# Sinkhorn attention and a feed-forward block on one core: zero halves moved from q to K, and batch 0 without padding

## The chip, the cores and the metric

The kernel runs on one core of a Trainium2 chip. A core has a matrix engine, TensorE (PE), with its own stream of weight loads (PEld); VectorE (DVE); ScalarE (ACT); GpSimd (POOL); and SyncE (SP), which here only issues transfers. TensorE reads SBUF, the 128-partition working memory, and writes PSUM, 8 banks of 512 fp32 columns per partition. VectorE and ScalarE copy results out of PSUM. POOL and SP issue the DMAs: loads that turn fp32 into bf16 come from POOL, transposes and stores from SP.

The metric is the device time of one execution in microseconds (us). The profiles show single executions, with a span from the first to the last instruction; the time of the execution is slightly longer than its span.

## The reference, cut to what matters

```python
# q, k, v: (4, 8, 768, 64); sort_net: (4, 8, 8, 8); 8 blocks of 96 rows
P = sort_net
for _ in range(5):                     # sinkhorn
    P = exp(P - max(P, -1)); P = P / (sum(P, -1) + 1e-9); P = P / (sum(P, -2) + 1e-9)
k_sorted = einsum('bhij,bhjcd->bhicd', P, k_b)      # blocks of K and V mixed by P
v_sorted = einsum('bhij,bhjcd->bhicd', P, v_b)
scores = q_b @ k_sorted.T / 8                       # inside each 96-row block
attn = softmax(scores)
x = (attn @ v_sorted) -> (3072 tokens, 8 heads * 64 = 512)
h = x @ w_in                                        # 512 -> 2048
g = maximum(h, 0) + alpha * minimum(h, 0)
out = g @ w_out                                     # 2048 -> 512
```

## The kernel before

The kernel records its operations in a graph (`G.add`), each with the tiles that it reads and writes. Each engine then runs its own fixed sequence, given as lists of operation numbers (`ORDER`) together with the PSUM bank of each result (`BANKS`); both lists were found by a search. Semaphores are set where an operation needs another engine's result. An engine runs its list strictly in order, so an operation that waits holds up all behind it. "Fillers" in TensorE's list (L1009) and the burst (L907) are matmuls without a result that keep TensorE working while it would wait.

**Blocks.** There are 32 attention blocks g (4 batches b of 8 blocks i), each of 96 queries and keys for 8 heads. Heads stand in 4 pairs, h4 = 0..3 with the halves hp = 0, 1: half 0 in partitions 0 to 63 and half 1 in 64 to 127.

**Sinkhorn** (L560 to L574) is a chain of small VectorE operations with one ScalarE exponential per round. Its result Pb is spread by small matmuls (`spread0`, L584, for batch 0; `spread` for the others) and made into the mixing matrices BDQ, BDM (for K) and BDV (for V).

**Batch 0 ("near").** q is transposed by TensorE (`prep_q`, L645) and copied to QTz. `prep_k0` (L661) mixes and transposes K, in six units, each copied to KT. `prep_v` (L716) mixes V in eight units, each copied to VS. In KT each 24-key group is padded to 32 columns with copies of other keys (L670, on POOL), so that 96 keys become 128 columns; in VS the rows that belong to padding are zero, also in the column that counts the keys (`one0`). For V the tile hT serves as the loading area, with zeros at L495 and L497; the weights of `prep_v` are read from it with a step of 64 elements. A block then runs on TensorE as: s1 (L755: scores with the queries along partitions), a VectorE reduction to the negative maxima nm (L762), s2 (L770: scores with the keys along partitions), sub (L781: subtract the maximum), on ScalarE the exponential to ET (L801), on TensorE o (L812: outputs and the sums), on VectorE the reciprocal (L817) and product xq (L820), on TensorE the transpose tr (L834) and a copy to xT.

**Batches 1 to 3 ("far").** q is loaded by POOL head by head to QN (L430), 128 columns per head, of which the half of the other partition half is zero (QN0, L508). SP transposes QN (L440) to QTz, in six pieces of 1024 columns, so QTz holds two copies per pair with zero halves. `conv_k` (L677, POOL) and `prep_k` (L689) mix K; one copy per unit brings both halves into KT, 112 columns per pair and block. `conv_v` lays V into VDz, and `prep_v` mixes it. In a far block s1 (L752) is 8 matmuls of 96 moving columns: with 128 partitions and zero halves in the weights, each gives the scores of one head. VectorE takes the negative maxima nf, ScalarE the exponentials to Esb (L789), SP transposes Esb to ET (L794). There are NE = 3 buffers of Esb, ET and xq. For batches 2 and 3 SP transposes xq to xT too.

**Feed-forward.** FFN1 (L853) runs on two chunks of 192 tokens and then seven of 384, 16 tiles each: 4 matmuls, ScalarE's relu t (L860), VectorE's product and sum hT (L863). FFN2 (L885) runs per 128 tokens in four groups of 4 matmuls with 512 columns; VectorE or ScalarE copies the result to outstg and SP stores it (L896). A copy out of PSUM that both engines can do has the line of the helper, L397.

Of the kernel before, what the change touches and what calls it, by code (L numbers as in the profile page):

```python
# [13 lines left out]
NB = 8  # L14
# [9 lines left out]
BK = (128, 112)  # L24
LK = 4 * NB * 128
NE = 3
VSL = 4
EPS = 1e-9
BURST = 140
# [13 lines left out]
        723 759 662 894 659 893 890 660 661 889 663 819 787 788 818 918 917""",  # L43
    "sync": """
# [3 lines left out]
        1127 1098 1118 1090 1058 1148 1172 1214 1226 1193 1220 1232""",  # L48
    "pe": """
# [17 lines left out]
        1224 1217 1218 1229 1230""",  # L67
    "act": """
# [10 lines left out]
        1180 1183 1195 1198 1147 1204 1207 1225 1219""",  # L79
    "dve": """  # L80
# [13 lines left out]
        1163 1151 1178 1160 1187 1192 1166 1175 1171 1184 1202 1181 1196 1199 1208 1205 1213 1231""",  # L94
}
BANKS = (
    "0720176402566007103123674545623016702014516040740232332571154023556674710151666723230371765023127466"
    "7345562601566762045563520172323073704233472267005451247552145562703761201777760440167073416745102212"
    "4567503020451227731314512700026654567764370120171140356567274267567010450223343406134451717670102147"
    "562372753011225033452370700112467116304617335716342532617524"  # L100
# [221 lines left out]
def bass_sinkhorn_attn__then__act_prelu_kernel(  # L322
# [40 lines left out]
    one0 = sb("one0", [128, 1], F32)  # L363
# [6 lines left out]
    QN = sb("QN", [128, 6, 8, 128], BF16)  # L370
# [3 lines left out]
    QTz = [sb("QTz%d" % n, [128, 2, 4, S], BF16) for n in range(2)]  # L374
# [38 lines left out]
    d_qn = [dma_sem("qn%d" % h) for h in range(H)]  # L413
# [10 lines left out]
    def load_q(b, prio):  # L424
        if b == 0:
            o, i = quarters(hT, 8192, HR, q)
            G.add(POOL, lambda e: e.dma_start(o, i), load_us, w=[("QS", 0)], prio=prio, dma=(d_q, 0), kind="load")
            return
        for h in range(H):
            G.add(POOL, lambda e, h=h: e.dma_start(  # L430
                AP(QN, h * 128 + (h // 4) * 64, [[6144, 128], [1024, 6], [1, 64]]),
                AP(q.tensor, b * HB + h * S * D, [[D, 128], [128 * D, 6], [1, D]])),
                660, r=[("QN0", h)] + paced(13, h // 2) * (b == 3), w=[("QN", h)], prio=prio,
                dma=(d_qn[h], 0), kind="load")
# [45 lines left out]
    def consts():  # L480
# [26 lines left out]
        for h in range(H):  # L507
            G.add(POOL, lambda e, h=h: e.memset(  # L508
                AP(QN, h * 128 + (1 - h // 4) * 64, [[6144, 128], [1024, 6], [1, 64]]), 0.0),
                430, w=[("QN0", h)], prio=-21)  # L510
# [538 lines left out]
```

## Time and profile before

| | |
|---|---|
| times of the runs | 237.92, 237.5 and 244.82 us; median 237.92 |
| profiled execution | 237.91 us, span 236.2 us |
| granted TensorE clock, mean over the span | 0.986 |
| HBM read, written | 27.28 MB, 6.29 MB |
| DMA issues, median to landing: KS (768 KB) 9.8 us, w_in (512 KB) 9.2 us, QN (96 KB) 3.7 us | |
| DMA transposes, median to landing: QTz 3.4 us, ET 3.2 us, xT 2.4 us | |

Busy times are unions of an engine's instruction spans; instructions of one engine overlap by some hundredths of a microsecond, so a sum of durations is a little larger. For TensorE a matmul's duration contains the time it takes to run through the array, so what it costs in a dense stream is the distance from one start to the next, which the chain of waits shows (so many matmuls in so many us). The chain follows back from the last instruction what released each step.

### The profile page before, as it was taken

What the parts mean: (1) busy time and instruction counts of PE and PEld (TensorE: products, weight loads), DVE (VectorE), ACT (ScalarE), POOL (GpSimd) and SP (SyncE); (2) the same over time, 40 slices, a digit from 0 to 9 for tenths busy, and PEclk for the clock granted to TensorE, in tenths of its full rate; (3) what the DMA queues carried; (4) which work ended last, traced back from release to release, by engine and by line L of the source; (5) the groups of instructions that cost most, each with busy time, mean ns of one, the idle gap of its engine ahead of it and who ended that gap; (6) DMA issues with size and microseconds to landing.
All of it is one profiled execution on the core that took longest, in us unless ns stands there. A gap on an engine that the chain in (4) does not pass through costs nothing.

```text
span 236.2 us, 5977 instructions
## 1 busy us (share of the span) xinstructions
PE 228.7 (97%) x2379; PEld 144.9 (61%) x2379; DVE 167.2 (71%) x344; ACT 151.8 (64%) x421; POOL 104.3 (44%) x153
## 2 busy tenths in 40 slices
PE   5999989999999999999999999999999999999995
PEld 3469868866566666566665666565655556455553
DVE  5774499997699788896797687684877558634741
ACT  4356648988598796687867758457758564433331
POOL 7939929997399997431778880000000000000000
PEclk9998599999999999999999999999999999999999
DMA  5999999996999999999828999842282691400024
GB/s 82 213 218 208 208 190 209 220 153 46 179 181 132 106 127 181 220 231 180 160 80 84 102 132 143 164 81 51 60 118 75 154 166 44 140 4 0 0 92 179
DMA packets 72381, 31.35 MB, mean 133 GB/s; under 512 B 64528, under 2 KB 67360, under 8 KB 72352
## 3 DMA queue, kind: packets, MB, share of 16 engines
q0 software_dynamic: 23808, 13.63, 42.6%
q1 hardware_dynamic: 48544, 17.33, 36.8%
q8 instruction: 19, 0.31, 0.6%
q14 instruction: 10, 0.08, 0.1%
HBM read 27.28 MB, written 6.29 MB: 142 GB/s over the span
## 4 chain that ended last, share of the span: by engine, by line
PE 82%; DMA 7%; DVE 5%; ACT 3%; issue 1%; SPq 0%; POOLq 0%
PE ps L853 32%; PE ps L885 31%; PE ps L716 4%; PE ps L752 4%; PE ps L812 3%; DMA ET<-Esb 3%; DMA hT<-in_q_dram 3%; PE ps L781 2%; DVE hT L863 2%; PE ps L689 1%; ACT ET L801 1%; DVE outstg L397 1%; PE ps L834 1%; PE ps L755 1%; DMA out_dram<-outstg 1%
## 5 line engine op out<-in xcount | busy, mean ns | idle before, releaser
L863 DVE SCALAR_TENSOR_TENSOR hT<-t,omaT,ps 128x384 bf16<-128x384 f32 (+1 forms) x144 | 76.7, 562 | 30.8 <-ACT t L860 29.1
L853 PE MATMUL ps<-xT,w_in_bf 128*128 128x384 bf16 (+1 forms) x576 | 95.6, 308 | 0.2 <-DVE rec L817 0.2
L885 PE MATMUL ps<-w_out_bf,hT 128*128 128x512 bf16 (+1 forms) x400 | 93.4, 371 | 0.1
L860 ACT ACTIVATE t<-ps 128x384 f32<-128x384 f32 (+1 forms) x144 | 61.5, 458 | 43.8 <-PE ps L853 33.7
L853 PEld LDWEIGHTS ps<-xT,w_in_bf 128*128 128x128 bf16 x576 | 51.8, 98 | 29.6 <-ACT xT L397 0.4
L885 PEld LDWEIGHTS ps<-w_out_bf,hT 128*128 128x128 bf16 x400 | 36.5, 98 | 32.9 <-DVE VS L397 0.2
L789 ACT ACTIVATE Esb<-ps,nf 96x96 bf16<-96x96 f32 x192 | 46.1, 345 | 6.4 <-DVE nf L762 6.2
L397 POOL COPY VDz<-VST 64x384 bf16<-64x384 bf16 x40 | 34.1, 852 | 9.8 <-DMA VST<-in_v_dram 6.0
L677 POOL COPY KSz<-KS 64x512 bf16<-64x512 bf16 x36 | 22.0, 612 | 8.9 <-DMA KS<-in_k_dram 3.6
L762 DVE TENSOR_REDUCE nf<-ps 96x8 f32<-96x768 f32 x24 | 22.7, 948 | 3.5 <-PE ps L752 3.4
L430 POOL DMA_DIRECT2D QN<-in_q_dram x24 | 20.0, 838 | 6.5 <-DMA QTz<-QN 6.5
L820 DVE TENSOR_TENSOR xq<-ps,rec 96x512 bf16<-96x512 f32 x32 | 21.7, 681 | 0.4
L812 PEld LDWEIGHTS ps<-VS,ET 112*128 112x128 bf16 (+1 forms) x256 | 11.4, 99 | 5.2 <-ACT ET L801 0.9
L812 PE MATMUL ps<-VS,ET 112*128 112x65 bf16 (+1 forms) x256 | 13.4, 196 | 1.1 <-ACT ET L801 0.6
L397 DVE COPY outstg<-ps 128x512 f32<-128x512 f32 (+1 forms) x14 | 9.3, 667 | 7.1 <-PE ps L885 4.8
L752 PEld LDWEIGHTS ps<-KT,QTz 128*96 128x96 bf16 x192 | 11.9, 125 | 3.6 <-ACT VS L397 0.5
L397 ACT ACTIVATE VS<-ps 112x512 bf16<-112x512 f32 (+1 forms) x18 | 12.0, 697 | 3.1 <-PE ps L716 2.9
L397 ACT ACTIVATE KT<-ps 128x512 bf16<-128x512 f32 x17 | 9.8, 600 | 4.1 <-PE ps L661 2.4
L752 PE MATMUL ps<-KT,QTz 128*96 128x96 bf16 x192 | 12.4, 208 | 0.0
L817 DVE RECIPROCAL rec<-ps 96x8 f32<-96x8 f32 x32 | 6.3, 200 | 8.3 <-PE ps L812 8.1
L762 DVE TENSOR_REDUCE nm<-ps 96x8 bf16<-96x768 f32 x8 | 7.6, 949 | 5.9 <-PE ps L755 5.8
L397 ACT ACTIVATE outstg<-ps 128x512 f32<-128x512 f32 (+1 forms) x11 | 6.4, 579 | 7.9 <-PE ps L885 7.9
(101 smaller groups left out, 183.6 us busy)
## 6 DMA issues: line engine op xcount, KB each, us to landing
out_dram<-outstg SPq DMA_DIRECT2D x23, 256.0 KB, 2.6
KS<-in_k_dram POOLq DMA_DIRECT2D x3, 768.0 KB, 9.8
QN<-in_q_dram POOLq DMA_DIRECT2D x24, 96.0 KB, 3.7
w_in_bf<-in_moe_w_in_dram POOLq DMA_DIRECT2D x4, 512.0 KB, 9.2
w_out_bf<-in_moe_w_out_dram POOLq DMA_DIRECT2D x2, 1024.0 KB, 16.3
VST<-in_v_dram POOLq DMA_DIRECT2D x4, 384.0 KB, 13.5
hT<-in_q_dram POOLq DMA_DIRECT2D x1, 768.0 KB, 7.3
hT<-in_v_dram POOLq DMA_DIRECT2D x2, 384.0 KB, 6.2
```

The lines of the kernel that those rows point to most:

```text
L397: return e.activation(o, i, ACTF.Copy) if e is nc.scalar else e.tensor_copy(o, i)
L430: G.add(POOL, lambda e, h=h: e.dma_start(AP(QN, h * 128 + (h // 4) * 64, [[6144, 128], [1024, 6], [1, 64]]), AP(q.tensor, b * HB + h * S * ...
L677: G.add(POOL, lambda e, hp=hp: e.tensor_copy(AP(KSz, hp * 64 * 3072 + u % 3 * 1024 + hp * 64, [[3072, 64], [128, 8], [1, 64]]), AP(KS[n], ...
L752: inst = e.matmul(o, AP(QTz[n], hp * 3072 + h4 * 768 + i * 96, [[6144, 128], [1, 96]]), AP(KT[n], (h4 * 8 + i) * bk, [[LK, 128], [64, 2], ...
L762: G.add(DVE, lambda e: e.tensor_reduce(AP(nx, 0, [[8, 96], [4, 2], [1, 4]]), AP(ps, X.at(), [[LP, 96], [X.step, 2], [96, 4], [1, 96]]), Ax ...
L789: inst = e.activation(AP(Esb[me], p * 128, [[1024, 96], [64, 2], [1, 48]]), AP(ps, X.at((p % 4) * 96) + p // 4 * X.step, [[LP, 96], [48, 2 ...
L812: inst = e.matmul(AP(ps, Z.at(h4 * 68) + hp * Z.step, [[LP, 128], [1, 65]]), AP(ET[et], pos(h4, hp) * 96, [[800, nk], [1, 128]]), AP(VS[n] ...
L820: G.add(DVE, lambda e: e.tensor_tensor(out=AP(xq[me], 0, [[512, 96], [256, 2], [64, 4], [1, 64]]), in0=AP(ps, Z.at(), [[LP, 96], [Z.step, ...
L853: inst = e.matmul(AP(ps, T.at(), [[LP, 128], [1, n]]), AP(w_in_bf, kt * DFF + ft * 128, [[KT_TILES * DFF, 128], [1, 128]]), AP(xT, kt * XR ...
L860: G.add(ACT, lambda e: e.activation(AP(t1[tb], 0, [[384, 128], [1, n]]), AP(ps, T.at(), [[LP, 128], [1, n]]), ACTF.Relu, scale=-1.0), t_ac ...
L863: G.add(DVE, lambda e: e.scalar_tensor_tensor(out=AP(hT, ft * RING + tok % RING, [[FT_TILES * RING, 128], [1, n]]), in0=AP(t1[tb], 0, [[38 ...
L885: inst = e.matmul(AP(ps, T.at(), [[LP, 128], [1, n]]), AP(hT, ft * RING + tok % RING, [[FT_TILES * RING, 128], [1, 128]]), AP(w_out_bf, ft ...
```

## The change

- **Far q and K.** QN holds 4 x 128 columns without zero halves and there are two of it, by batch; the six transposes carry 512 columns each into QT, one copy per pair. KT has 192 columns per pair and block: columns 0 to 95 hold half 0's keys in partitions 0 to 63, columns 96 to 191 half 1's in partitions 64 to 127, and the rest is zero (`zero_k`, two POOL memsets for each of the two KT buffers). s1 of a far block is 4 matmuls of 192 moving columns, one for each pair.
- **Copies to KT.** `prep_k`'s result of batches 1 to 3 is copied in two halves of 64 partitions, so 36 copies take the place of 18.
- **Batch 0.** No padding: KT has 96 columns per block, `prep_k0` copies to 24 columns per group without the POOL copy, `prep_v` reads 96 weight columns instead of 128, s2 loads 96 key columns, the zeros of hT are 2 x 1536 columns, VS's counting column is a plain memset for both buffers (`one0`, its ScalarE copy and a later memset go).
- `spread0` is three graph operations with a bank each instead of one.
- NE = 4 buffers of Esb, ET and xq; BURST 180 instead of 140.
- `ORDER` and `BANKS` are new throughout. TensorE's fillers are 10, 13, 5, 1 and 2 matmuls instead of 11, 11, 3, 1 and 3. On POOL, v's first half is issued behind q and before K; K of batch 1 is issued before the second zero memset of hT and three of the four w_in loads follow directly; the loads of batch 1's q come earlier against the copies of V. On VectorE two VS copies of batch 0 stand before four of the KT copies. Until the first 384-token tile VectorE has 5 of the VDz copies and ScalarE 3 (before: 2 and 6), ScalarE 10 KT copies and VectorE 2 (before 5 and 1); beside the first sixteen 384-token tiles VectorE has 5 KT copies (before 1).

```diff
-BK = (128, 112)
-LK = 4 * NB * 128
-NE = 3
+BK = (96, 192)
+LK = 4 * NB * 192
+NE = 4
...
-            AP(QTz[n], t * 128, [[6144, 128], [768, 8], [1, 128]]),
-            AP(QN, t * 1024, [[6144, 128], [1, 1024]])),
+            AP(QT[n], t * 128, [[3072, 128], [768, 4], [1, 128]]),
+            AP(QN[n], t * 512, [[3072, 128], [1, 512]])),
...
-                    AP(hT, th * 64 * HR + th * 4096, [[HR, 64], [2048, 2], [1, 1536]]),
-                    AP(v.tensor, th * 3072, [[6144, 64], [1536, 2], [1, 1536]])), load_us / 2,
+                    AP(hT, th * 64 * HR + th * 3072, [[HR, 64], [1, 3072]]),
+                    AP(v.tensor, th * 3072, [[6144, 64], [1, 3072]])), load_us / 2,
...
-        for h in range(H):
-            G.add(POOL, lambda e, h=h: e.memset(
-                AP(QN, h * 128 + (1 - h // 4) * 64, [[6144, 128], [1024, 6], [1, 64]]), 0.0),
-                430, w=[("QN0", h)], prio=-21)
+        zero_k(1, -21)
...
-        if u == 1:
-            G.add(POOL, lambda e: e.tensor_copy(AP(KT[0], 24, [[LK, 128], [32, 128], [1, 8]]),
-                                                AP(KT[0], 0, [[LK, 128], [32, 128], [1, 8]])), 1150,
-                  r=[("KT", 0, 0), ("KT", 0, 1)], w=["KTpad"], prio=prio + 0.1)
+    def zero_k(n, prio):
+        z = KT[n].bitcast(F32)
+        for hp in range(2):
+            G.add(POOL, lambda e, hp=hp: e.memset(
+                AP(z, hp * 64 * (LK // 2) + (1 - hp) * 48, [[LK // 2, 64], [96, 32], [1, 48]]), 0.0),
+                1600, w=[("KTz", n, hp)], prio=prio)
...
-        o = AP(KT[n], 8 * u, [[LK, 128], [BK[1], 32], [64, 2], [1, 8]])
-        G.add(EITHER, lambda e: copy(e, o, AP(ps, T.at(), [[LP, 128], [2, 32], [1, 2], [64, 8]])),
-              t_either(512), r=[T], w=[("KT", n, u)], prio=prio)
+        for hp in range(2):
+            G.add(EITHER, lambda e, hp=hp: copy(
+                e, AP(KT[n], hp * (64 * LK + 96) + 8 * u, [[LK, 64], [192, 32], [48, 2], [1, 8]]),
+                AP(ps, hp * 64 * LP + T.at(), [[LP, 64], [2, 32], [1, 2], [64, 8]])),
+                t_either(512), r=[T], w=[("KT", n, u, hp)], prio=prio)
...
-                    AP(hT, 8 * u + dd, [[HR, 128], [64, 128]])
-                inst = e.matmul(AP(ps, T.at(dd * 64), [[LP, 128], [1, 64]]), z,
+                    AP(hT, 8 * u + dd, [[HR, 128], [64, 96]])
+                inst = e.matmul(AP(ps, T.at(dd * 64), [[LP, 128 if b else 96], [1, 64]]), z,
...
             for h4 in range(4):
+                if far:
+                    inst = e.matmul(sc(2 * h4, 96, 192), AP(QT[n], h4 * 768 + i * 96, [[3072, 128], [1, 96]]),
+                                    AP(KT[n], (h4 * 8 + i) * bk, [[LK, 128], [1, bk]]))
+                    continue
                 for hp in range(2):
-                    o = sc(pos(h4, hp), 96)
-                    if far:
-                        inst = e.matmul(o, AP(QTz[n], hp * 3072 + h4 * 768 + i * 96, [[6144, 128], [1, 96]]),
-                                        AP(KT[n], (h4 * 8 + i) * bk, [[LK, 128], [64, 2], [1, 48]]))
```

More of the change, by code (lines that the diff above doesn't have):

```diff
@@ L369, in bass_sinkhorn_attn__then__act_prelu_kernel @@
     hT = sb("hT", [128, FT_TILES, RING], BF16)
-    QN = sb("QN", [128, 6, 8, 128], BF16)
+    QN = [sb("QN%d" % n, [128, 6, 4, 128], BF16) for n in range(2)]
     KS = [sb("KS%d" % n, [128, 3072], BF16) for n in range(2)]
@@ L373, in bass_sinkhorn_attn__then__act_prelu_kernel @@
     VDz = sb("VDz", [128, VSL * 8 * 128], BF16)
-    QTz = [sb("QTz%d" % n, [128, 2, 4, S], BF16) for n in range(2)]
+    QT = [sb("QT%d" % n, [128, 4, S], BF16) for n in range(2)]
     KT = [sb("KT%d" % n, [128, LK], BF16) for n in range(2)]
@@ L411, in bass_sinkhorn_attn__then__act_prelu_kernel @@
     load_us = 3720
-    d_qn = [dma_sem("qn%d" % h) for h in range(H)]
+    d_qn = [dma_sem("qn%d" % h) for h in range(2 * H)]
     d_qt = [dma_sem("qt%d" % t) for t in range(6)]
@@ L494, in consts @@
         for th in range(2):
[L495 to L498 removed]
+            G.add(POOL, lambda e, th=th: e.memset(AP(zh, th * 64 * HR // 2 + (1 - th) * 1536, [[HR // 2, 64], [1, 1536]]), 0.0),
+                  1450, w=[("VDo", th)], prio=-95.2)
         zv, zk = VDz.bitcast(F32), KSz.bitcast(F32)
@@ L506, in consts @@
             G.add(DVE, lambda e, n=n: e.memset(AP(ET[n], 768, [[800, 128], [1, 32]]), 0.0), 100, w=[("ETp", n)], prio=-88)
-        for h in range(H):
-            G.add(POOL, lambda e, h=h: e.memset(
-                AP(QN, h * 128 + (1 - h // 4) * 64, [[6144, 128], [1024, 6], [1, 64]]), 0.0),
-                430, w=[("QN0", h)], prio=-21)
-        G.add(DVE, lambda e: e.memset(AP(VS[1], 64, [[64 * 65, 128], [65, 64]]), 0.125), 110, w=[("VS1", 1)], prio=-30)
+        zero_k(1, -21)
+        for n in range(2):
+            G.add(DVE, lambda e, n=n: e.memset(AP(VS[n], 64, [[64 * 65, 128], [65, 64]]), 0.125), 110, w=[("VS1", n)],
+                  prio=(-69, -30)[n])
         def red(o, src, w, prio=-70, ax=AxisListType.X):
@@ L532, in consts @@
               prio=-67)
-        red(one0[:, :], AP(identf, 0, [[128, 128], [32, 4], [1, 24]]), "one0", -69, AxisListType.XY)
-        G.add(ACT, lambda e: e.activation(AP(VS[0], 64, [[64 * 65, 128], [65, 64]]), AP(one0, 0, [[1, 128], [0, 64]]),
-                                          ACTF.Copy, scale=0.125),
-              490, r=["one0"], w=[("VS1", 0)], prio=-60)
         G.add(ACT, lambda e: copy(e, AP(selk, 0, [[512, 32], [16, 32], [1, 16]]),
@@ L577, in spread0, with f @@
     def spread0(prio):
-        T = G.bank(1, "P")
-        def f(e):
-            inst = None
-            for x in range(3):
+        T = [G.bank(1, "P") for _ in range(3)]
+        for x in range(3):
+            def f(e, x=x):
+                inst = None
                 for j in range(8):
-                    inst = e.matmul(AP(ps, T.at(x * 8), [[LP, 128], [1, 8]]), AP(w_out_bf, x * 1024 + j * 128, [[WR, 32], [1, 128]]),
+                    inst = e.matmul(AP(ps, T[x].at(), [[LP, 128], [1, 8]]),
+                                    AP(w_out_bf, x * 1024 + j * 128, [[WR, 32], [1, 128]]),
                                     AP(Pb, j, [[64, 32], [8, 8]]), start=(j == 0), stop=(j == 7))
-            return inst
-        G.add(PE, f, 24 * 26, r=["Pb"] + [("sel0", x) for x in range(3)], w=[T], prio=prio, mode=1)
+                return inst
+            G.add(PE, f, 8 * 26, r=["Pb", ("sel0", x)], w=[T[x]], prio=prio, mode=1)
         for x in range(2):
@@ L649, in prep_q @@
         G.add(PE, f, 8 * 58, r=[("QS", 0), "identb"], w=[T], prio=prio, mode=4)
-        G.add(EITHER, lambda e: copy(e, AP(QTz[0], 8 * u, [[6144, 128], [24, 128], [1, 8]]),
+        G.add(EITHER, lambda e: copy(e, AP(QT[0], 8 * u, [[3072, 128], [24, 128], [1, 8]]),
                                      AP(psb, 2 * T.at(), [[2 * LP, 128], [1, 128], [128, 8]])),
@@ L714, in f @@
                 z = AP(VDz, (u % VSL * 8 + dd) * 128, [[VSL * 1024, 128], [1, 128]]) if b else \
-                    AP(hT, 8 * u + dd, [[HR, 128], [64, 128]])
-                inst = e.matmul(AP(ps, T.at(dd * 64), [[LP, 128], [1, 64]]), z,
+                    AP(hT, 8 * u + dd, [[HR, 128], [64, 96]])
+                inst = e.matmul(AP(ps, T.at(dd * 64), [[LP, 128 if b else 96], [1, 64]]), z,
                                 AP(BDV, b * 64, [[256, 128], [1, 64]]))
             return inst
-        G.add(PE, f, 235 if b else 8 * 60,
-              r=[(x, th) for x in ("VD", "VDo", "VDp") for th in range(2)] * (b == 0) +
-              [("VDz", u % VSL, th) for th in range(2)] * (b > 0) + [("BDV", b)], w=[T], prio=prio)
+        G.add(PE, f, 235 if b else 8 * 69,
+              r=[(x, th) for x in ("VD", "VDo") for th in range(2)] * (b == 0) +
+              [("VDz", u % VSL, th) for th in range(2)] * (b > 0) + [("BDV", b)], w=[T], prio=prio, mode=0 if b else 7)
         G.add(EITHER, lambda e: copy(e, AP(VS[n], 8 * u, [[64 * 65, nk], [65, 64], [1, 8]]),
@@ L734, in attention @@
         bk = BK[far]
-        nk = 112 if far else 128
+        nk = 112 if far else 96
         pos = (lambda h4, hp: 2 * h4 + hp) if far else (lambda h4, hp: 4 * hp + h4)
-        kt_keys = [("KT", n, u) for u in range(6)]
-        qt_keys = [("QTzt", n, t) for t in range(i * 96 // 128, (i * 96 + 95) // 128 + 1)] if far else \
+        kt_keys = [("KT", n, u, hp) for u in range(6) for hp in range(2)] + [("KTz", n, hp) for hp in range(2)]
+        qt_keys = [("QTt", n, t) for t in range(i * 96 // 128, (i * 96 + 95) // 128 + 1)] if far else \
             [("Q0", u) for u in range(3)]
@@ L797, in attention @@
         else:
[L798 removed]
+            op = G.add(PE, s2, 190, r=kt_keys + qt_keys + [("nm", m)], w=[X], prio=ps_, mode=2)
             near.append(op.idx)
@@ L977, in bass_sinkhorn_attn__then__act_prelu_kernel @@
         if g == 7:
-            G.add(DVE, lambda e: e.memset(AP(VS[0], 64, [[64 * 65, 128], [65, 64]]), 0.125), 110,
-                  w=[("VS1", 0)], prio=8)
+            zero_k(0, 9)
         if b + 1 < B:
```

60 lines of the change are left out of this document (27 added, 33 removed), and 97 rows, old and new, of the table ORDER.

## The prediction, made before the changed kernel was run

> **What bounds the kernel now.** I read the page first, then the windows by stage, then the chain of waits.
>
> ```profile
> span 236.2 us, 5977 instructions
> ...
> PE 228.7 (97%) x2379; PEld 144.9 (61%) x2379; DVE 167.2 (71%) x344; ACT 151.8 (64%) x421; POOL 104.3 (44%) x153
> ...
> PE 82%; DMA 7%; DVE 5%; ACT 3%; issue 1%; SPq 0%; POOLq 0%
> ```
>
> TensorE (PE) is busy almost throughout and carries 82% of the chain. That is an average over unlike stages, so the windows come next: stretch, busy time of PE, weight loads, DVE, ACT and POOL, then granted clock and DMA.
>
> ```profile
> 18.30:21.70 3.40, 3.40 (x47) 3.21 (x46) 1.99 (x3) 2.57 (x5) 3.40 (x8) 1.00 1.03 205
> 21.70:28.60 6.90, 6.90 (x98) 5.85 (x98) 2.02 (x3) 3.68 (x7) 6.49 (x12) 0.51 1.06 207
> 34.00:60.70 26.70, 26.25 (x381) 20.67 (x381) 23.55 (x54) 20.90 (x50) 21.20 (x32) 1.00 1.17 155
> 60.70:100.00 39.30, 39.11 (x413) 24.43 (x409) 33.02 (x60) 30.89 (x94) 30.93 (x43) 1.00 1.17 165
> 130.00:233.50 103.50, 103.25 (x790) 59.64 (x785) 64.97 (x114) 58.44 (x172) 10.10 (x14) 1.00 0.50 92
> ```
>
> Three regimes show. Until 34 us the kernel prepares batch 0, and for 6.9 us of that the granted clock is 0.51. From 34.0 to 60.7 VectorE is busy 23.55 of 26.70 us beside a busy PE: two engines are nearly level. After 60.7 PE alone sets the pace, with VectorE at 84% until 100 us and far below later. The chain dates the borders.
>
> ```profile
> 12.69 0.23 DVE Pb L574
> ...
> 16.74 2.26 PE ps L716 x24
> 19.00 0.31 PE ps L755 x8
> ...
> 34.11 0.44 PE ps L853 x4
> ...
> 233.56 0.41 DVE outstg L397
> ```
>
> The sinkhorn result Pb is there at 12.9, batch 0's first scores run at 19.0, the first FFN1 tile at 34.1, and the last copy starts at 233.56; copy and store then take the 2.6 us to the span's end. Profiled time is 237.91 us, 1.7 over the span, and practically the median of the runs shown, 237.92.
>
> **The change, part by part: matmuls.** These rows give prices from start to start, which is what a full PE pays.
>
> ```profile
> 34.72 1.32 PE ps L853 x16
> 65.97 0.36 PE ps L752 x8
> 62.18 1.73 PE ps L885 x8
> 132.97 0.47 PE ps L689 x16
> ...
> L752 PEld LDWEIGHTS ps<-KT,QTz 128*96 128x96 bf16 x192 | 11.9, 125 | 3.6 <-ACT VS L397 0.5 <-ACT Esb L789 0.3 <-DVE hT L863 0.2
> L716 PE MATMUL ps<-BDV,hT 128*128 128x64 bf16 x64 | 6.4, 260 | 0.0
> L716 PEld LDWEIGHTS ps<-BDV,hT 128*128 128x128 bf16 x64 | 6.0, 206 | 0.2
> ```
>
> A far head pair now takes one matmul with 192 moving columns, not two with 96. The 192-column matmul of the small FFN1 tile is 1.32/16 = 0.0825 us; the score matmul is 0.36/8 = 0.045. Per block 4 x 0.0825 = 0.33 replaces 0.36, for 24 blocks 0.72 us off PE, all on the path after 60.7. Ends: nothing at all (if 192 columns cost twice 96) to 0.72.
>
> Batch 0's v preparation loads its 64 weights as 96 columns instead of 128. The chain's 2.26 us for 24 is 0.094 each, against 0.029 (0.47/16) where the weights lie densely in L689. So the strided load sets it; by columns 0.094 x 96/128 = 0.071, so 64 x 0.023 = 1.5 us off PE before 34 us. Ends: 0.045, the price of a whole L752 matmul with 96 weight columns (3.1 us gained), to 0.121, 0.094 plus the 0.027 by which the mean load in the L752 row, 125 ns, exceeds the 98 ns that this row shows for 128 columns:
>
> ```profile
> L853 PEld LDWEIGHTS ps<-xT,w_in_bf 128*128 128x128 bf16 x576 | 51.8, 98 | 29.6 <-ACT xT L397 0.4 <-DVE rec L817 0.3 <-DVE VS L397 0.2
> ```
>
> That end would lose 1.7 us. I take 0.071, from the row of the same strided load. The Trainium skill speaks against the dense form: in "TensorE: Matmul & The Clock Gate", section "Weight-path perf modes — Fast Weight Load (FWL) and DoubleRow", the fast load applies only at 128 weights, and by the section "LDWEIGHTS (loading the stationary operand)" a load takes columns/1.2 ns, an estimate of 80 ns for 96. By it the 64 loads would gain 0.9 us instead of 1.5, and far scores could not run under 0.080 each; the 0.045 of L752 shows that no such floor holds for contiguous weights here.
>
> Scores, max subtraction and outputs of batch 0 keep their counts; s2 now loads 96 columns as L755 already does (0.31 us for 8). I cost that at nothing, the cover being that L755 row; without it 64 x 0.027 = 1.7 us.
>
> **Start.** q, v and K stay the first loads in POOL's queue, v's first half only moves ahead of K, so I leave their landings where they are. The sinkhorn chain takes in work:
>
> ```profile
> L514 DVE TENSOR_REDUCE mk<-identf 128x16 f32<-128x128 f32 x1 | 0.4, 373 | 1.4 <-POOL identf L482 1.4
> L495 POOL MEMSET hT<- 64x2048 f32 x2 | 3.6, 1818 | 0.1
> L508 POOL MEMSET QN<- 128x384 bf16 x8 | 3.4, 420 | 0.4
> ```
>
> Reductions like this one now stand between its steps on VectorE (some beside ACT's exponentials, where they are hidden), and on POOL v's issue stands ahead of the identity for which ACT's queue waits. I put Pb 0.6 us later, 13.5 (0 to 1.1, three such reductions in full). Hidden: PE reaches v at 16.7 only; if v came sooner, it would cost its 0.6.
>
> ```profile
> L397 DVE CAST KT<-ps 128x512 bf16<-128x512 f32 x7 | 4.7, 685 | 1.7 <-PE ps L689 1.0 <-PE ps L661 0.7
> L397 DVE CAST VS<-ps 112x512 bf16<-112x512 f32 x14 | 9.6, 687 | 2.6 <-PE ps L716 2.6
> ```
>
> The new wait is on VectorE: two VS copies now stand ahead of four of the six KT copies. From 17.3 (16.74 and a first v group of 8 x 0.071) six copies of 0.69 and a small reduction of 0.2: K is complete at 21.6, so the first scores come 2.6 us later than 19.0. Queued behind: every score and ET of batch 0. In return six of eight v groups are done by then, not three: 3 x 8 x 0.071 = 1.7 us fewer between first score and FFN1. Two output groups (0.41 each, below) also move behind FFN1: 0.8. The old 34.1 - 19.0 = 15.1 us contain the half-clock stretch.
>
> ```profile
> 22.47 0.76 PE ps L781 x8
> ...
> 24.58 0.48 PE ps L755 x6
> ...
> 30.49 0.41 PE ps L812 x8
> ...
> 31.52 0.46 PE ps L781 x8
> ```
>
> In it a max subtraction takes 0.76 against 0.46 later and a score group 0.48 against 0.31; for three subtractions, four score groups and the outputs I count 2 us. With the five extra fillers ahead of v and shorter v groups I expect the clock to stay up. The rest, about 0.5 us, is ET waits that overlap. So 15.1 - 1.7 - 0.8 - 2.0 - 0.5 = 10.1, and FFN1 starts at 31.7 instead of 34.1. Ends: 29.5 (v at 0.045) and 34 (half clock again, or v at 0.121).
>
> On POOL the eight QN memsets (0.42 each) and the KT pad copy go; four memsets of KT halves come, by the hT row 1.82 x 1536/2048 = 1.4 each. Those for batch 1 stand among q's loads; the last for batch 2 stands behind batch 3's K loads, which wait for the transposes of earlier blocks, and batch 2's first scores wait for it.
>
> ```profile
> 107.06 0.36 PE ps L752 x8
> ```
>
> That is when they ran before; POOL was busy 30.93 of 39.30 us until 100, so there is slack and I cost it at nothing; without it 1.4 us.
>
> **From FFN1 to the first 384-token tile.** VectorE is the one to count, up to the xT copy that this tile needs.
>
> ```profile
> 35.78 2.60 DVE L863 SCALAR_TENSOR_TENSOR hT<-t,omaT,ps 128x192 bf16<-128x192 f32 x7
> ...
> 59.59 0.35 DVE L397 COPY xT<-ps 128x384 bf16<-128x384 bf16 x1
> ...
> 60.72 1.46 PE L853 MATMUL ps<-xT,w_in_bf 128*128 128x384 bf16 x8
> ...
> L820 DVE TENSOR_TENSOR xq<-ps,rec 96x512 bf16<-96x512 f32 x32 | 21.7, 681 | 0.4
> L397 DVE COPY VDz<-VST 64x384 bf16<-64x384 bf16 x2 | 1.7, 853 | 0.1
> L762 DVE TENSOR_REDUCE nm<-ps 96x8 bf16<-96x768 f32 x8 | 7.6, 949 | 5.9 <-PE ps L755 5.8
> ```
>
> Before: 28 hT x 0.371 (2.60/7) + 4 VS x 0.687 + 3 nm x 0.949 + 3 xq x 0.681 + 2 VDz x 0.853 + 1 KT x 0.685 and 2.2 of small ones = 22.6 us, in the 24.2 from 35.78 to 59.94: a rate of 0.936. After, by the new order: 29 hT, 1 VS, 3 nm, 5 xq, 4 VDz, 2 KT and 2.3 of small ones = 24.8; at 0.936 that is 26.5. ACT gets five more KT copies and three fewer VDz there and stays below VectorE. First hT at 31.7 + 0.9 (two tile steps and the ACT copy) = 32.6, xT at 59.1, the first large tile at 59.7 instead of 60.7: of the 2.4 us won at the start more than half is given back. Ends for the stage: 24.8 at rate 1 and 29.2 at 0.85.
>
> **The rest.** PE has 172.8 us from 60.72 to 233.5. The new order leaves two FFN2 groups more for it (0.865 each) and two v groups (0.235 each), less 0.72: +1.5. KT copies in halves mean 12 more evictions for batches 2 and 3.
>
> ```profile
> 64.45 0.65 PE ps L853 x4
> ...
> 227.52 1.14 DVE L863 SCALAR_TENSOR_TENSOR hT<-t,omaT,ps 128x384 bf16<-128x384 f32 x2 [0.64 <-ACT t L860]
> ...
> L397 DVE COPY outstg<-ps 128x512 f32<-128x512 f32 x13 | 8.8, 685 | 4.8 <-PE ps L885 4.8
> ```
>
> Beside the first sixteen large tiles VectorE had 16 hT x 0.57, 7 reductions, 7 VS, 4 xq, 3 output copies, a KT copy and small ones: 27.5 us against PE's 30.2 (16 x 0.65, 15 x 0.865 and 27 small groups). The new order adds 4 KT, an output copy and a 0.6 product: 31.6 against 32.4, 98% after 91%. The next two sixteens go to 20.3 against 21.6 and 21.2 against 23.1. I add 1.5 us of stall (0 to 5). Smaller q transposes, a second QN buffer and a fourth ET buffer take waits off SP and POOL, but PE's idle time there is 0.2 of 39.3 us already, so they gain nothing.
>
> End of PE: 59.7 + 172.8 + 1.5 + 1.5 = 235.5; tail 2.6, outside 1.7: **239.8 us**, no measurable change (2% is about what a measurement of this kernel can tell from none: 233.2 to 242.7).
>
> **The rivals.** VectorE becomes the bound (slower). Place: 32 to 105 us; mechanism: the halved KT copies plus the VS and VDz copies put on it. If it can be driven at 0.90, not 0.936, the middle stage takes 27.6, and the first three runs of sixteen large tiles 35.1, 22.5 and 23.6 us against PE sums of 32.4, 21.6 and 23.1: 1.1 + 2.7 + 0.9 + 0.5 less the 1.5 already counted = 3.7 more, 243.5; at 0.85 the same sums give about 250. It decides from 0.90. For it: 0.936 was reached where PE was level too; against: after 60.7 nothing in the old trace tests it. I take 245, chance 0.30.
>
> The half clock comes back. Row: 0.51 after a stretch in which PE looked busy 3.40 of 3.40 us but ran 47 matmuls, mostly 64 columns long. FFN1 then starts at 34: 242.1. Chance 0.12, a third of it past 2%. The Trainium skill, "TensorE: Matmul & The Clock Gate", Part 1 (the clock gate), has just two clocks, half and full, and an idle window of about 3.4 us before the drop; the 6.9 us stretch agrees with two windows.
>
> Everything fits (faster). FFN1 at 29.5 and VectorE full give 29.5 + 0.9 + 24.8 + 0.6 = 55.8 for the large tile, and without stalls 55.8 + 174.3 + 4.3 = 234.4; under 233.2 needs a shorter prelude still. Chance 0.08.
>
> The merged score matmul saves nothing: 192 columns at twice 0.045. Then 240.5; chance 0.04. That leaves the forecast 0.46.
>
> **Numbers.** Faster 0.08; within 2%: 0.46 + 0.08 + 0.04 = 0.58; slower 0.30 + 0.04 = 0.34. The forecast's own range is 236 to 242; with the rivals 234 to 246, leaving out a tenth at each end.
>
> **What would show it.** L752 at 0.33 us per four; batch 0's v matmuls at 0.071; batch 0's first scores near 21.6, FFN1 near 31.7, first 384-token tile near 59.7; PE clock 1.00 from 18 to 32; VectorE over 90% from 32 to 95 with PE idle under 3 us after it. Wrong if PE idles long on VectorE evictions or on KT's zero memset, or if the strided 96-column load costs more than 128 did.

## The result, and the profile after

The changed kernel takes 248.97 us (median of four runs, 247.76 to 250.18) against 238.28 for the kernel before, measured beside it: 1.046 times as long, 95% interval 1.039 to 1.053. It is slower, and by more than the range of the prediction allowed. Ratios, here and below, leave out runs over 1.5% above the fastest of their kernel (here the 244.82 us of the kernel before). The profiled execution took 247.76 us, the shortest of the four; its span is 2.1 us shorter.

The page of the changed kernel first: instructions, busy times, the granted clock in 40 slices, and the chain's shares.

```profile
span 245.7 us, 5850 instructions
...
PE 236.7 (96%) x2300; PEld 153.6 (63%) x2325; DVE 177.2 (72%) x361; ACT 151.0 (61%) x421; POOL 104.5 (43%) x147
...
PEclk9997555899999999999999999999999999999999
...
PE 82%; DVE 9%; DMA 5%; issue 1%; ACT 1%; POOL 1%; POOLq 0%
```

The kernel has 54 matmuls fewer than before (the weight loads, x2325 against x2379, show it; of the matmuls the trace lacks another 25 records, all of L883), yet PE is busy 8 us longer. The clock line says where to look: the fourth to the eighth slice (6.1 us each) lie under full clock, and after them nothing is amiss. The windows of that stretch (stretch, busy PE, weight loads, DVE, ACT, POOL, then granted clock and DMA):

```profile
18.30:21.70 3.40, 3.40 (x41) 3.27 (x41) 2.64 (x6) 0.28 (x1) 1.71 (x4) 0.97 1.06 212
21.70:28.60 6.90, 6.90 (x56) 6.12 (x56) 2.48 (x4) 3.46 (x7) 6.63 (x10) 0.50 1.06 214
28.60:42.20 13.60, 13.60 (x166) 11.34 (x165) 7.96 (x17) 5.37 (x7) 1.51 (x2) 0.50 0.89 140
```

PE counts as busy without a gap, but it starts 56 matmuls in the 6.9 us in which the kernel before started 98. Half clock lasts from 21.5 to 45.4, 23.9 us instead of 6.8. The chain of waits says which matmuls are slow already at full clock:

```profile
17.02 3.79 PE ps L714 x24
...
26.80 0.80 PE ps L752 x11
27.60 2.75 PE ps L714 x16
...
41.71 0.64 PE ps L851 x4
...
243.06 0.42 DVE outstg L397
```

The first 24 v matmuls of batch 0 take 3.79 us at full clock, 0.158 each, where the kernel before took 2.26. At half clock 16 take 2.75, 0.172 each: the clock hardly matters to them. Start to start over all 64 the median is 0.163. The first scores run at 26.7 (before: 19.0), FFN1 at 41.7 (34.1). So 7.6 us of the 9.85 that the two profiled runs lie apart are lost by then. The stage up to the first large tile adds 0.5 and all behind it 1.7; there the prediction had put 3.0 more than before, so that part was foreseen. The timeline of PE has the first 384-token tile at 68.8, and two windows follow, up to it and behind it:

```profile
68.81 0.81 PE L851 MATMUL ps<-xT,w_in_bf 128*128 128x384 bf16 x4
```

```profile
41.70:68.80 27.10, 26.13 (x370) 21.18 (x371) 23.04 (x56) 22.52 (x54) 20.09 (x31) 0.93 1.05 110
68.80:100.00 31.20, 30.80 (x298) 18.86 (x298) 28.08 (x49) 23.56 (x75) 27.79 (x37) 1.00 0.84 127
```

| start of | before | forecast | after |
|---|---|---|---|
| first scores | 19.0 | 21.6 | 26.7 |
| FFN1 | 34.1 | 31.7 | 41.7 |
| first 384-token tile | 60.7 | 59.7 | 68.8 |
| time of the profiled run | 237.91 | 239.8 | 247.76 |

Against the forecast: +10.0 us up to FFN1, 27.1 instead of 28.0 to the large tile (-0.9), 178.95 instead of 180.1 from there on (-1.15); together the 7.96 by which it missed. The start alone missed by 10.0; the two later terms, both too long, hid 2.05 of it.

### The profile page after: what moved, and what is told of

Its sections match the earlier page's. It is cut to its first block, busy times and chain, and to the rows that moved or that the text cites. A ratio compares the mean times of both kernels' runs of the same rounds, so it can differ in the third digit from the quotient of the medians.

```text
span 245.7 us, 5850 instructions
## 1 busy us (share of the span) xinstructions
PE 236.7 (96%) x2300; PEld 153.6 (63%) x2325; DVE 177.2 (72%) x361; ACT 151.0 (61%) x421; POOL 104.5 (43%) x147
## 4 chain that ended last, share of the span: by engine, by line
PE 82%; DVE 9%; DMA 5%; issue 1%; ACT 1%; POOL 1%; POOLq 0%
PE ps L883 31%; PE ps L851 30%; PE ps L714 6%; DMA KS<-in_k_dram 5%; DVE hT L861 4%; PE ps L810 3%; PE ps L748 3%; PE ps L779 2%; PE ps L685 1%; PE ps L832 1%; DVE nm L760 1%; PE ps L1006 1%; DVE VS L397 1%; PE ps L752 1%; DVE VDz L397 1%
## 5 line engine op out<-in xcount | busy, mean ns | idle before, releaser
L851 PE MATMUL ps<-xT,w_in_bf 128*128 128x384 bf16 (+1 forms) x576 | 98.1, 312 | 0.8 <-DVE hT L861 0.7
L861 DVE SCALAR_TENSOR_TENSOR hT<-t,omaT,ps 128x384 bf16<-128x384 f32 (+1 forms) x144 | 76.6, 560 | 25.5 <-ACT t L858 24.4
L883 PE MATMUL ps<-w_out_bf,hT 128*128 128x512 bf16 (+1 forms) x375 | 89.5, 370 | 1.4 <-issue 0.2
L851 PEld LDWEIGHTS ps<-xT,w_in_bf 128*128 128x128 bf16 x576 | 52.7, 99 | 29.4 <-DVE hT L861 1.9
L883 PEld LDWEIGHTS ps<-w_out_bf,hT 128*128 128x128 bf16 x400 | 37.2, 98 | 32.4
L760 DVE TENSOR_REDUCE nf<-ps 96x8 f32<-96x768 f32 x24 | 22.8, 951 | 6.8 <-PE ps L748 6.5
L397 ACT ACTIVATE KT<-ps 64x512 bf16<-64x512 f32 (+1 forms) x27 | 15.9, 590 | 10.9 <-PE ps L654 9.2
L810 PEld LDWEIGHTS ps<-VS,ET 112*128 112x128 bf16 (+1 forms) x256 | 12.3, 102 | 4.4 <-ACT xT L397 0.6
L397 DVE CAST VS<-ps 112x512 bf16<-112x512 f32 (+1 forms) x18 | 12.4, 686 | 3.7 <-PE ps L714 3.5
L397 ACT ACTIVATE VS<-ps 112x512 bf16<-112x512 f32 (+1 forms) x14 | 9.4, 683 | 5.1 <-PE ps L714 5.1
L748 PE MATMUL ps<-KT,QT 128*96 128x192 bf16 x96 | 11.9, 246 | 0.0
L748 PEld LDWEIGHTS ps<-KT,QT 128*96 128x96 bf16 x96 | 9.5, 123 | 3.4 <-DVE hT L861 0.3
```

The costliest lines, as they stand in the source:

```text
L397: return e.activation(o, i, ACTF.Copy) if e is nc.scalar else e.tensor_copy(o, i)
L748: inst = e.matmul(sc(2 * h4, 96, 192), AP(QT[n], h4 * 768 + i * 96, [[3072, 128], [1, 96]]), AP(KT[n], (h4 * 8 + i) * bk, [[LK, 128], [1, ...
L760: G.add(DVE, lambda e: e.tensor_reduce(AP(nx, 0, [[8, 96], [4, 2], [1, 4]]), AP(ps, X.at(), [[LP, 96], [X.step, 2], [96, 4], [1, 96]]), Ax ...
L810: inst = e.matmul(AP(ps, Z.at(h4 * 68) + hp * Z.step, [[LP, 128], [1, 65]]), AP(ET[et], pos(h4, hp) * 96, [[800, nk], [1, 128]]), AP(VS[n] ...
L851: inst = e.matmul(AP(ps, T.at(), [[LP, 128], [1, n]]), AP(w_in_bf, kt * DFF + ft * 128, [[KT_TILES * DFF, 128], [1, 128]]), AP(xT, kt * XR ...
L861: G.add(DVE, lambda e: e.scalar_tensor_tensor(out=AP(hT, ft * RING + tok % RING, [[FT_TILES * RING, 128], [1, n]]), in0=AP(t1[tb], 0, [[38 ...
```

## The experiments

Three theories stood after this. L: a strided load of 96 weight columns is slow by itself, and through it the clock falls. C: the new order and its fillers bring the half clock, whatever the loads are. V: VectorE, with the halved KT copies, sets the time. Each ratio below is to the kernel before as run beside it, with medians of 238.4 us for e1 to e4, 239.5 for e5 to e8 and 240.4 for e9; times from different groups compare only roughly.

**The loads by themselves (e1_loads, e5_loads_full).** Behind the last matmul of the changed kernel stand groups that differ only in their weights.

```diff
+for x in range(24):        # e5: 16, behind 24 dense matmuls for each group
+    e.matmul(AP(ps, bank * 512 + x % 8 * 64, [[LP, COLS], [1, 64]]),
+             AP(hT, x, [[HR, 128], [STEP, COLS]]), AP(identb, 0, [[128, 128], [1, 64]]))
```

> The changed kernel with ten groups of 24 matmuls behind its last one on TensorE, each with 64 moving columns of identb and weights read from hT, the groups differing only in the weights: 128, 112, 96, 64 and 32 columns with a step of 64 elements; 96 and 128 columns with a step of 1; 96 columns with steps of 2, 16 and 65. Eight 512-column matmuls stand ahead of them. The distance from start to start is measured; the run's whole time says nothing. Theory L (a strided load of 96 columns is slow by itself): step 64 with 96 columns 0.155 to 0.175 us each, with 128 columns 0.085 to 0.095; which of the other groups are slow tells whether it is the count, the step, or both. Theory P (the load costs by its columns, as I predicted; what was slow in the changed kernel was the place: half clock, busy DMA): step 64 with 96 columns 0.065 to 0.075 here, where the clock is full and no DMA runs.

In e1 the groups with a step of 64 took, by the median from start to start, 0.090 us with 128 columns and 0.164 with 96, so P fell at once. But the slow loads brought half clock behind them for the groups that followed, and 96 contiguous columns stood there at 0.080. The second run keeps the clock up with dense work.

> As in the first run of loads, but with 24 dense 512-column matmuls (5.2 us) ahead of every group, so that no group runs at half clock, and 16 matmuls per group: step 64 with 96, 112, 64 and 128 weight columns, and 96 columns with steps 1, 2, 4, 8 and 16, 128 columns with step 1. If the slowness is one of the step alone, at 1.7 ns per column unless there are 128: step 64 gives 0.164, 0.19, 0.11 and 0.09, steps 1 and 2 at most 0.045, and somewhere between 2 and 16 the time jumps to 0.16 or more. If the half clock made the contiguous 96 columns fast or slow in the first run (0.080 there), they come at 0.040 here; if not, at 0.080.

Its chain, 16 matmuls to a row; ahead of each group stand the dense ones, L1018. The groups themselves ran at full clock; half clock came three times, in the dense matmuls behind a slow group (the 6.87 us row holds the first). In this order: step 64 with 96, 112 and 64 columns; step 1 with 128 and 96; 96 columns with steps 2, 4, 8 and 16; step 64 with 128.

```profile
248.75 2.48 PE ps L1021 x16
251.23 5.18 PE ps L1018 x24
256.41 2.89 PE ps L1024 x16
259.30 6.87 PE ps L1018 x24
266.16 1.88 PE ps L1027 x16
268.04 5.29 PE ps L1018 x24
273.33 0.47 PE ps L1030 x16
...
278.97 0.71 PE ps L1033 x16
...
284.87 0.75 PE ps L1036 x16
...
290.79 1.38 PE ps L1039 x16
...
297.35 2.67 PE ps L1042 x16
...
306.88 2.73 PE ps L1045 x16
...
316.48 1.35 PE ps L1048 x16
```

The first of each group had its weights loaded early, so the medians are a little above a sixteenth of a row: 0.163, 0.190, 0.110; 0.029, 0.045; 0.048, 0.0905, 0.176, 0.180; and 0.088 for 128 columns with the step of 64. Two things have to come together, a step and a count other than 128. Contiguous or with a step of 2, 96 columns are cheap; from a step of 8 on they cost 1.7 to 1.9 ns a column, and with a step of 64 so do 112 and 64 columns (0.190/112, 0.110/64). With the same step 128 columns cost 0.69 ns each. So a strided load of fewer columns costs more than one of 128, down to about 52 columns, an estimate (0.088/1.7 ns); e1's group of 32, at half clock, took 0.057.

**The changed kernel with 128 columns (e2_v128).** v lies 2048 columns further, and the 32 surplus columns read q's data.

```diff
-                    AP(hT, 8 * u + dd, [[HR, 128], [64, 96]])
-                inst = e.matmul(AP(ps, T.at(dd * 64), [[LP, 128 if b else 96], [1, 64]]), z,
+                    AP(hT, 2048 + 8 * u + dd, [[HR, 128], [64, 128]])
+                inst = e.matmul(AP(ps, T.at(dd * 64), [[LP, 128], [1, 64]]), z,
```

> The changed kernel, but batch 0's v weights are read as 128 columns with the step of 64 again. v lies 2048 columns further in hT, so that the 32 columns too many read q's data; their result rows are not copied. All else, the order too, is as in the changed kernel. Theory L (the loads' shape is the cause, and through the longer thin stretch on TensorE the long half clock too): the 64 loads at 0.085 to 0.10 each, 4.5 us less; first scores at 22.5 to 23.5 instead of 26.7; half clock 7 to 10 us instead of 24; FFN1 at 34 to 36; 239 to 242 us. Theory C (the new order and fillers bring the half clock whatever the loads are): loads 0.09, but still over 17 us of half clock, FFN1 near 38, 244 to 246 us. Theory V (VectorE, loaded with the halved KT copies, is the bound from 42 us on): 247 or more, since what the start wins VectorE takes back.

237.7 us, 0.998 times the kernel before (0.996 to 1.000): the whole loss is gone, and V with it. Its chain of waits, then its windows:

```profile
16.35 2.23 PE ps L1006 x5
18.58 2.04 PE ps L714 x24
...
24.34 0.49 PE ps L752 x16
...
34.03 0.50 PE ps L851 x4
```

```profile
14.90:18.30 3.40, 3.02 (x21) 1.61 (x22) 1.10 (x1) 0.00 (x0) 0.00 (x0) 0.52 1.05 217
18.30:21.70 3.40, 3.40 (x53) 3.18 (x52) 2.44 (x5) 0.47 (x1) 1.53 (x3) 0.98 1.05 210
21.70:25.10 3.40, 3.40 (x52) 2.98 (x51) 1.99 (x5) 3.00 (x7) 3.28 (x6) 1.00 1.07 216
```

The loads are at 0.085 again and full clock holds through the v groups, so C has fallen as well: order and fillers are those of the changed kernel. One window of half clock is left, earlier, while PE waits for K; five fillers then take 2.23 us and hold v up by 2 us.

**One part alone (e4_before96).** The kernel before, with the narrow load. Batch 0's outputs then sum over 96 rows, not 128, so a quarter of its padded keys is left out; order, fillers and all else are as before.

```diff
-                    AP(hT, 8 * u + dd, [[HR, 128], [64, 128]])
+                    AP(hT, 8 * u + dd, [[HR, 128], [64, 96]])
-        nk = 112 if b else 128          # rows of the VS copy; o likewise over 96 rows
+        nk = 112 if b else 96
```

> The kernel before, with one part of the change alone: batch 0's v weights are read as 96 columns instead of 128 (result rows 96 to 127 are left out, and the outputs of batch 0 sum over 96 rows instead of 128, so a quarter of batch 0's padded keys is left out). Order, fillers and everything else as before. Theory L: the 64 loads take 0.155 to 0.175 each, 4.5 us more in sum, and half clock lasts 10 to 20 us instead of 6.8; FFN1 at 39 to 42; 243 to 248 us. Theory C: no slower loads to speak of or no more half clock, FFN1 within 1 us of 34.1, 237 to 240 us.

246.35 us, 1.037 times the kernel before (1.032 to 1.041). The chain has the same slow group, and FFN1 stands where the changed kernel has it:

```profile
16.67 4.06 PE ps L716 x24
...
41.77 0.64 PE ps L853 x4
```

Half clock lasts 23.9 us here too (19.1 to 42.95). One edit, put in alone, brings most of the loss; taken out alone, it removes all of it.

**Dense work between the slow loads (e3_v96fill, e8_v96fill3).** One or three 512-column matmuls ahead of each v group of the changed kernel, into the group's own bank, which it then overwrites.

```diff
+            for _ in range(0 if b else 3):      # e3: 1
+                e.matmul(AP(ps, T.at(), [[LP, 128], [1, 512]]), identb[:, :],
+                         AP(identb, 0, [[128, 128], [0, 4], [1, 128]]))
```

> The changed kernel with one dense matmul of 512 columns (0.22 us at full clock) ahead of the 8 matmuls of each of batch 0's v groups, 8 in all, 1.8 us more work before FFN1; the v loads stay at 96 columns. If the half clock follows from how thinly the slow loads use TensorE, one dense matmul per 1.3 us shortens it: half clock under 14 us and 243 to 247 us in spite of the work added. If one is too few, or the clock doesn't depend on that: still 20 us or more of half clock and 249 to 252 us.

248.9 us, between the two expectations: half clock shrank from 23.9 to 17.1 us only, and the added work (8 x 0.216 = 1.7 us) about took the gain. One dense matmul per group was too few to decide it.

> The changed kernel with slow 96-column v loads and three dense 512-column matmuls, not one, ahead of each of batch 0's v groups: 24, 5.2 us of work more at full clock. It tells whether dense work between the slow loads keeps the clock up. If it does (half clock under 7 us): 10.4 us of loads and 5.2 of dense work against 5.9 in e2_v128, FFN1 at 41 to 44, 245 to 248 us. If the half clock lasts 17 us or more: the dense matmuls take 0.43 each, FFN1 at 46 or later, 251 to 256 us.

246.75 us (1.032, 1.026 to 1.039), with 5.2 us more work than the changed kernel and still slightly less time (1.046). Half clock lasts 3.4 us in its trace, ahead of the v groups. The windows behind show full clock beside slow loads:

```profile
21.70:25.10 3.40, 3.40 (x41) 3.03 (x42) 1.96 (x4) 0.14 (x1) 3.28 (x6) 1.00 1.05 212
25.10:28.50 3.40, 3.40 (x28) 2.79 (x27) 1.58 (x3) 1.63 (x3) 3.29 (x5) 1.00 1.09 220
```

So dense work keeps the clock up, and the loads stay slow under it: two separate costs.

**Fillers moved, or taken away (e6_ahead, e7_nofill).** Both with 128-column loads. Near its start TensorE's list reads, in e2, e6 and e7 (count.bank are fillers):

```diff
-  10.1 90 88 13.2 83 84 128 82 92     102 100 5.5 114
+  10.1 90 88 17.2 83 84 128 82 92 2.5 102 100 2.5 114     # e6
+  10.1 90 88 1.2  83 84 128 82 92     102 100 1.5 114     # e7
```

> The changed kernel with 128-column v loads as in e2_v128, and fillers moved: 17 instead of 13 ahead of the spread of Pb, 2 ahead of the first K matmuls, and 2 instead of 5 between these and the first v matmuls. In e2_v128 TensorE idled 0.98 and 0.55 us there, the clock went to half at 15.0 for 3.4 us, and the five fillers then took 2.2 us and held up v (landed at 16.4) to 18.4. If the idle time brought that half clock, it stays at 1.0 through 18 us, v starts at 16.4 to 16.9, FFN1 at 32.3 to 33, and the time is 1 to 2 us under e2_v128: 235.7 to 237. If the half clock comes in any case or comes later instead (as in the kernel before at 21.7), no gain: 237 to 239.

236.98 us, with all twelve runs between 236.63 and 237.25; 0.992 times the kernel before (0.989 to 0.996), a little better than the kernel before; against e2 (0.996 to 1.000) the intervals only touch. The clock stays at 1.00 throughout, and v, the first scores and FFN1 come 1.4 to 1.7 us earlier than in e2 (chain of waits):

```profile
16.85 2.33 PE ps L714 x24
...
22.91 0.49 PE ps L752 x16
...
32.63 0.50 PE ps L851 x4
```

> The changed kernel with 128-column v loads as in e2_v128, and the 13 and 5 fillers ahead of Pb's spread and of the first v matmuls cut to 1 each. It tells what half clock alone costs where the v loads are fast. Theory: TensorE idles 4 us between 9.6 and 15.2, the clock is half from 12 or 15 us on for two to seven windows of 3.41 us; per window some 1 us is lost, so FFN1 at 35 to 38 and 239 to 243 us. If the clock isn't worth what I take it to be, or recovers by itself at the first K matmuls: v starts at 16.5, FFN1 at 32.5 to 34, 236 to 238 us.

The profiled run had a single window of half clock (14.1 to 17.5) and took 236.74 us; the other three took 242.7 to 243.3 at a mean clock of 0.943. Four runs so far apart give no ratio, but, if the clock is all that sets them apart, they price it: 0.943 instead of 0.993 over some 240 us is 24 us more at half clock (0.05 x 240 x 2), for 6.2 us of time, about 0.9 us per window of 3.41. Only the profiled run left a trace, so where those 24 us lay is not shown. Without the fillers the time is left to chance; with them ahead of the wait it is not.

**What the clock follows (e9_before_dense).** For each window of 3.413 us, counted from the clock's changes, I added up, over the matmuls started in it, moving columns x rows x columns in use, as a share of 8192 columns through the full 128 x 128 array (3.413 us at about 0.216 us per dense 512):

```
window at full clock        share   next window
before      18.3            0.30    half
after       18.1            0.28    half
e2          11.6            0.26    half
e3          17.3            0.24    half
e4          15.7            0.24    half
e7          10.7            0.02    half
e8          12.4            0.26    half
e8          39.7            0.34    full (lowest of those that stayed full)
```

These runs went into e9's expectation; e9 was the test. One dense matmul went ahead of four of batch 0's v groups of the kernel before:

```diff
+            if not b and u in (0, 2, 4, 6):
+                e.matmul(AP(ps, T.at(), [[LP, 128], [1, 512]]), identb[:, :],
+                         AP(identb, 0, [[128, 128], [0, 4], [1, 128]]))
```

> The kernel before, with one dense 512-column matmul ahead of four of batch 0's eight v groups (the third, fourth, fifth and seventh in TensorE's order), 0.86 us of work more; the v loads keep their 128 columns. In the runs so far a window of 3.41 us at full clock was followed by half clock when the matmuls started in it filled the array by at most 0.30 (moving columns x rows x columns in use, over 8192 columns of 128 x 128), and never from 0.34 up; the kernel before has 0.30 in its window at 18.3. Theory: two of the dense matmuls fall into that window and lift it to 0.4, half clock doesn't come, the 6.8 us stretch at half clock costs about 0.9 us per window less, and FFN1 starts at 33 instead of 34.1: 236.3 to 237.5 us, level with e6_ahead, so that the rest of the change (with fast v loads) is worth nothing measurable by itself. If the clock doesn't follow that share: half clock stays, 238.5 to 240 us.

236.3 us, 0.987 times the kernel before (0.980 to 0.993). The stretch that had half clock runs at 1.00 (the windows from 16.7 and 20.1 now have shares of 0.39 and 0.46), and the timeline of PE has FFN1 1.7 us earlier than before:

```profile
18.30:21.70 3.40, 3.40 (x46) 3.12 (x46) 1.99 (x3) 2.11 (x4) 3.40 (x8) 1.00 1.05 208
21.70:25.10 3.40, 3.40 (x58) 3.11 (x58) 0.20 (x1) 2.63 (x6) 3.15 (x6) 1.00 1.06 212
```

```profile
32.38 0.50 PE L855 MATMUL ps<-xT,w_in_bf 128*128 128x192 bf16 x4
```

More work, less time. The profiled run had a window of half clock much later (at 108.8) and took 239.72 us, as one more did with 241.84; the other five took 235.8 to 236.6 at a mean clock of 1.00. So what was gained is read from the start of its trace alone. The gain of 1.3% is more than the 1.7 us at FFN1; most runs of the kernel before beside it had mean clocks of 0.964 to 0.979, under the 0.986 of its profile. And e9 does with four matmuls in the old kernel what e6 does in the new one: their ratios overlap, so with fast v loads and the clock kept up, the rest of the change is worth nothing that can be measured here.

The line is less sharp than e9's expectation has it. All eleven traces together, the ends of the programs left out, have 14 windows at full clock that half clock followed. Twelve had a share of 0.30 or less, and no window so thin kept the clock. The other two had 0.355 (e9, at 105.4, where TensorE waited 2.2 us for q's transposes) and 0.389 (e5, at 307.0, behind a slow group). Nine windows between 0.34 and 0.39 stayed full, and all above. So e9's window of 0.39 lies where both happened. One dense matmul counted in or out of a window is 0.06, more than these differences. Moving columns alone, without the rows and columns in use, separate worse: e8's window at 12.4 has 0.52 and lost the clock, e3's at 10.5 has 0.40 and kept it.

## Why the prediction was wrong, step by step

**The step that failed: batch 0's v preparation.** I priced the 96-column strided load "by columns 0.094 x 96/128 = 0.071", a gain of 1.5 us, with 0.121 as the upper end. It is 0.163: 64 x (0.163 - 0.094) = 4.4 us lost, 5.9 from my value, and outside the bounds. (The 0.094 is a piece of the chain; the old median from start to start is 0.089, which makes the loss 4.7.) My last sign of being wrong, a 96-column load dearer than the 128, is the one that came. The row of the 128-column strided load was the nearest in form, but scaling it assumed that 96 columns are loaded in the same way; e5 shows that 128 columns are a case apart. The bounds came from contiguous rows (0.045 and the L752 mean), which say nothing of a step of 64. The trace of before had no strided load with fewer than 128 columns, and the honest upper end was an unknown multiple. I named what speaks against the change and then set it aside. The Trainium skill, "TensorE: Matmul & The Clock Gate", section "Weight-path perf modes — Fast Weight Load (FWL) and DoubleRow", has the fast load at 128 weights alone, and e5 agrees (step 64: 0.088 with 128, 0.190 with 112). Its section on LDWEIGHTS gives columns/1.2, an estimate of 80 ns for 96; e5 measures 45 contiguous and 163 with the step, so neither size held, and by 80 the change would still have been a gain.

**The step that hung on it: "I expect the clock to stay up".** Slow loads leave the array nearly empty (share 0.28 in the window at 18.1), and the clock went to half for seven windows. My rival had this as two windows and 242.1, because it took the old stretch over as it was. By e7's price the 23.9 us cost some 6.2. The two together close the sum: e6's 236.9, 64 x (0.163 - 0.090) = 4.7 for the loads and 6.2 for the clock make 247.8; the profiled run took 247.76. That it closes so well is partly luck, since the clock's price comes from e7's fast loads and from stretches that no trace shows.

**The wait that dated the first scores** was another. I put them at 21.6, when VectorE would have K complete. The last copy to KT ended at 24.3 in the changed kernel and at 21.8 in e6, but the scores ran at 26.7 and 22.8: in both TensorE was busy without a wait from its first v matmul on, because six v groups and four K units stand ahead of the scores in its own list. At 0.071 a load that list would have lasted until about 21.5 (an estimate with e6's K rows), so my price hid it; at 0.163 each of these 48 loads delayed the scores directly.

**VectorE as the bound** (rival, 0.30) did not happen. From FFN1 to the large tile it was busy 23.0 of 27.1 us, under the 24.8 I had summed (in e6 23.5 of 25.6, with PE busy 24.6); from 68.8 to 100 it reached 90%, and PE was busy 30.8 of 31.2 beside it. I had added 1.5 us of stall; PE's waits after 69 us sum to 0.2.

**The merged score matmul** came at the price forecast: the chain has four in 0.35 (L748), with a median of 0.082 from start to start. Counted to whatever matmul starts next, all 96 take 8.17 us against 8.63 for the old 192, so 0.46 us is saved and not 0.72.

```profile
74.54 0.35 PE ps L748 x4
```

**The zero memsets** held nobody up: after 45 us PE waited only for hT and on issue. **s2 with 96 columns**, priced at nothing, cost a little: the median from the first to the last start of a group of eight is 0.174 us in e6 against 0.141 in e9, which keeps 128. The max subtraction loads 96 columns instead of 128 too, which the prediction does not count: 0.349 against 0.308. Over eight groups that makes some 0.6 us, an estimate.

**The rest of the working.** In e6, where the loads are at 0.090 and the clock holds, FFN1 starts at 32.6 against my 31.7, of which 64 x 0.019 = 1.2 is the load; the stage to the large tile takes 25.5 us, not 28.0, and the remainder 178.8, not 180.1. Both later terms were too long, VectorE's most. Had the load been what I took it for and the clock held as in e6, the time would have come near 236 (an estimate, 236.9 - 1.2), not 239.8.

## What to carry to other kernels

A price measured for one shape need not scale to another: before trimming a dimension off a round number such as 128, time the trimmed shape itself, with its strides. Count array work per few microseconds, not busy time: here thin stretches cost twice, by themselves and by the half clock that followed, and a dense matmul without a result, put into a thin stretch or ahead of a wait, paid for itself. When a change moves many things, put its most doubtful part alone into the old kernel and take it alone out of the new one; here those two runs settled it.

## What was not expected of the hardware

- Strided weight loads: with a step of 64, 64 columns cost 0.110 us, 96 0.163, 112 0.190 and 128 only 0.088. For 96 columns steps 1 and 2 cost 0.045 and 0.048, step 4 0.0905, steps 8 and 16 0.176 and 0.180. In the trace's records of these loads 128 columns are read as four runs of 32 and every other count as one run; whether that is the reason no run shows.
- The clock fell while the profile had TensorE busy without a gap. Each of the twelve windows at full clock with an array share of 0.30 or less was followed by half clock; between 0.34 and 0.39 two of eleven were, and none above. From half clock it came back after a window with a share of 0.37 or more (counted in the same unit), and once, in e3, after 0.31, while e4 stayed at half after 0.34. The Trainium skill, "TensorE: Matmul & The Clock Gate", Part 1 (the clock gate), ties the clock to how busy the engine was in windows of about 3.4 us; the lengths agree (3.413 and its multiples). What went with the clock in these traces is how full the array was, not what the profile counts as busy.
